# Moving the query copies ahead of a sine piece on GpSimd in a fused linear-attention and MLP kernel, with four smaller reorderings

## The chip, the cores and the metric

The kernel runs on one core of one Trainium2 chip. The metric is the device time of one execution in microseconds (us), as the median of several runs. A run's span in the profile is about 1.8 us shorter than its device time, because the profile counts from the first to the last instruction.

The engines are called as the profile calls them: PE is TensorE, DVE is VectorE, ACT is ScalarE, POOL (or Pool) is GpSimd, and SP issues the output stores. All five run at once, each in its own program order. They wait for one another only through semaphores.

## The reference

```python
# q, k, v: [8 batches, 8 heads, 576 positions, 64]
r = maximum(x, 0);  phi(x) = concat(r * cos(theta), r * sin(theta))   # theta grows with position
kv  = sum_s phi(k)[s] (x) v[s];  z = sum_s phi(k)[s]
x   = (phi(q) @ kv) / (phi(q) @ z + 1e-6)          # [4608, 512]
out = softplus(x @ w_in) @ w_out                   # w_in [512, 2048], w_out [2048, 512]
```

The kernel folds `w_in @ w_out` into one 512 x 512 matrix `W_c` and a bias, since softplus is almost linear for so small an argument. It checks the bound for that at the end; the check needs one sum of squares per tile, called norm `i`, which ScalarE computes, or VectorE for the tiles listed in `NORMS_DVE`. After the fold each of the 36 tiles of 128 tokens costs a few short PE groups.

## The kernel before

Per batch there is preparation: the values `v` are scaled by cos and by sin (`vcs`), the keys go through relu, and the queries are copied into another order (`q_r`). VectorE scales all cos pieces; the sin pieces are divided between VectorE and Pool. Then PE sums the key products of the batch. Per tile `i` there is the following, with PE's groups in this order:

```python
attend(i)          # PE: num_ps += qT[i] x kvblk;  DVE: rden = 1/den, x = num * rden
transpose(i - 1)   # PE: xT_ps <- x
keys(b)            # PE: 72 matmuls kv_ps <- vcs, k_sb, in the tile before the batch's first
emit(i - 4)        # PE: o_ps <- W_c, xT_all;  DVE: o_sb = o_ps + bias;  SP: store
turn(i + 2)        # PE: qT_ps <- diag, q_r (2 matmuls per query half);  ACT: qT = relu(qT_ps)
# then what the schedule has put into slot i, the end of tile i's work: prepare(...) of a later batch
```

The preparation that the change touches (cut; "..." marks cuts):

```python
def values_pool(b, hp, behind):          # one sin piece on Pool, 128 x 576
    ins = POOL.tensor_mul(vcs_bufs[b % 2][:, hp, :, 1, 0:D], raw["v", b][:, hp]..., cs_tab[:, 1])
    follow(ins, behind)                  # Pool waits until instruction `behind` has ended

def prepare(b, n):                       # slot first[b] - 6 + n for batches from 4 on
    if b < 4:
        ...
    else:
        if n < 3:
            relu_k(b) if n == 2 else values(b, 0, 2 * n)
        values_pool(b, n, None if n == 3 else before)   # before: the latest output add
        if n > 1:
            order_q(b, n - 2, POOL)      # query half n - 2, 128 x 576 int32
    if n == (2 if b < 4 else 3) and b + 3 < B:
        for name in ("v", "k", "q"):
            load(name, b + 3)
```

The output tiles `o_sb` form a ring of `OUTS = 16`, so output add n + 16 needs store n to have landed. The first stores are held back for loads:

```python
AHEAD = [("q", 5), ("v", 6), ("k", 6), ("q", 6), ("v", 7), ("k", 7)]   # store i waits for load AHEAD[i]
```

## Time and profile before

| | before |
|---|---|
| device time, median of 3 runs | 140.41 us (140.26 to 142.16) |
| span of the profile | 138.9 us |
| busy: PE, DVE, ACT, POOL | 82%, 71%, 71%, 56% |
| granted TensorE clock | 0.985 of full speed |

The profile is of another execution, which took 140.84 us. No engine is full on average, and the DMA engines are full until about 107 us. The averages therefore do not name the bound; it has to be read stage by stage.

The tables below use one more number, the lead. For tile n it is the time at which PE starts the tile's `attend` group in the profile of before, less that time in another profile. Positive means that the other kernel is ahead by so much. The column "end" is the last tile, 35. The places where the lead changes are the places where time is won or lost.

### The profile page before, as it was taken

Reading aid. Unit: us, or ns where it says so; the run is one execution under the profiler, and the core shown is the slowest. Engines: PE = TensorE matmul, PEld = TensorE weight load, DVE = VectorE, ACT = ScalarE, POOL = GpSimd, SP = SyncE. Lnnn points to the kernel's source line nnn. Section 1 sums busy time; section 2 is a strip of 40 time slices with the busy share of each in tenths; the row PEclk is TensorE's granted clock in tenths of the full one; section 3 lists DMA queues with packets and bytes.
Section 4 is the critical chain, followed back from the end, with each engine's and each line's share of the span. In section 5 each row is a group of like instructions: output and inputs, shape, how many; then the busy total and the mean of one; then the engine's idle time right before and its main releaser. Section 6 shows DMA issues by size and latency. Waiting matters only on the chain. (4 is left out here: it accounts for less than half of the span.)

```text
span 138.9 us, 3838 instructions
## 1 busy us (share of the span) xinstructions
PE 114.2 (82%) x1544; PEld 77.3 (56%) x1562; DVE 98.4 (71%) x205; ACT 98.5 (71%) x182; POOL 77.3 (56%) x81
## 2 busy tenths in 40 slices
PE   0199989999996776899899699789979987999910
PEld 0035775545444465676677477567747756776500
DVE  5184384335999599599599949959994896789720
ACT  3497873999841767888979579749949876899400
POOL 6964069993392519578568986915893591000000
PEclk9999999999999999999999999999999999999995
DMA  1999999999999999999999999999999432123570
GB/s 11 177 208 206 207 194 204 206 206 209 207 207 209 207 207 208 213 204 208 207 210 205 207 240 239 240 239 265 389 389 393 153 146 88 75 103 119 216 249 5
DMA packets 22676, 28.06 MB, mean 202 GB/s; under 512 B 1152, under 2 KB 18560, under 8 KB 22656
## 3 DMA queue, kind: packets, MB, share of 16 engines
q0 software_dynamic: 16896, 18.35, 78.4%
q1 hardware_dynamic: 5760, 9.44, 18.5%
q8 instruction: 13, 0.21, 0.6%
q14 instruction: 7, 0.06, 0.1%
HBM read 36.70 MB, written 9.44 MB: 332 GB/s over the span
## 5 line engine op out<-in xcount | busy, mean ns | idle before, releaser
L38 ACT ACTIVATE qT<-qT_ps 128x1024 bf16<-128x1024 f32 (+1 forms) x37 | 36.9, 1003 | 17.0 <-PE qT_ps L38 16.8
L38 POOL TENSOR_TENSOR vcs<-v_sb,cs_tab 128x576 bf16<-128x576 bf16 x22 | 35.2, 1602 | 16.6 <-DVE o_sb L38 12.4
L38 PE MATMUL o_ps<-W_c,xT_all 128*128 128x512 bf16 (+1 forms) x134 | 35.5, 373 | 0.9 <-issue 0.3
L38 DVE TENSOR_TENSOR o_sb<-o_ps,b_bc 128x512 f32<-128x512 f32 (+1 forms) x37 | 24.7, 671 | 9.2 <-PE o_ps L38 8.8
L38 PE MATMUL qT_ps<-diag,q_r 128*128 128x256 bf16 x144 | 22.5, 273 | 7.2 <-POOL q_r L38 5.1
L38 DVE TENSOR_TENSOR x<-num_ps,rden 128x512 bf16<-128x512 f32 x36 | 24.9, 692 | 3.5 <-ACT junk L38 0.6
L38 PE MATMUL num_ps<-kvblk,qT 128*128 128x130 bf16 (+1 forms) x320 | 22.8, 220 | 0.8 <-ACT qT L38 0.6
L38 PEld LDWEIGHTS <-q_r 128*128 128x128 bf16 x144 | 13.5, 98 | 17.1 <-POOL q_r L38 6.7
L38 ACT COPY xT_all<-xT_ps 128x1024 bf16<-128x1024 bf16 (+1 forms) x19 | 18.3, 961 | 2.5 <-PE xT_ps L38 2.5
L38 DVE TENSOR_TENSOR vcs<-v_sb,cs_tab 128x1152 bf16<-128x1152 bf16 x21 | 19.8, 961 | 0.2 <-DMA v_sb<-in_v_dram 0.2
L38 PEld LDWEIGHTS <-xT_all 128*128 128x128 bf16 x148 | 12.9, 98 | 10.4 <-issue 0.8
L38 PEld LDWEIGHTS <-qT 128*128 128x128 bf16 (+1 forms) x320 | 17.0, 99 | 1.3 <-ACT qT L38 1.0
L38 ACT ACTIVATE junk<-x 128x512 bf16<-128x512 bf16 x26 | 16.3, 627 | 0.0
L38 PEld LDWEIGHTS <-ones_bf 128*128 128x128 bf16 x94 | 9.6, 103 | 11.0 <-issue 7.9
L38 PE MATMUL wc_ps<-w_out_sb,wT 128*128 128x512 bf16 x61 | 14.6, 379 | 0.1
L38 PE MATMUL xT_ps<-order,x 128*128 128x128 bf16 x144 | 13.9, 219 | 0.9 <-DVE rden L38 0.3
L38 ACT CAST kvblk<-kv_ps 64x520 bf16<-64x520 f32 x16 | 9.5, 594 | 6.5 <-PE kv_ps L38 6.4
L38 PE MATMUL busy_ps<-cs_tab,ones_bf 128*128 128x512 bf16 x17 | 6.7, 557 | 6.4 <-ACT cs_tab L38 6.3
L38 PE MATMUL kv_ps<-vcs,k_sb 64*64 64x130 bf16 x576 | 10.1, 221 | 1.8 <-DVE k_sb L38 1.8
L38 DVE COPY wT<-wT_ps 128x512 bf16<-128x512 bf16 x16 | 6.0, 418 | 7.5 <-PE wT_ps L38 4.2
L38 DVE RECIPROCAL rden<-num_ps 128x8 f32<-128x8 f32 x36 | 7.3, 202 | 5.7 <-PE num_ps L38 5.6
L38 PEld LDWEIGHTS <-x 128*128 128x128 bf16 x144 | 9.8, 97 | 2.4 <-issue 1.7
(62 smaller groups left out, 131.9 us busy)
## 6 DMA issues: line engine op xcount, KB each, us to landing
out_dram<-o_sb SPq DMA_DIRECT2D x32, 256.0 KB, 3.8
v_sb<-in_v_dram POOLq DMA_DIRECT2D x8, 576.0 KB, 15.8
k_sb<-in_k_dram POOLq DMA_DIRECT2D x8, 576.0 KB, 18.3
q_sb<-in_q_dram POOLq DMA_DIRECT2D x8, 576.0 KB, 20.4
w_in_sb<-in_moe_w_in_dram POOLq DMA_DIRECT2D x4, 512.0 KB, 16.7
w_out_sb<-in_moe_w_out_dram POOLq DMA_DIRECT2D x4, 512.0 KB, 18.6
out_dram<-o_sb SPq DMA_DIRECT2D x8, 128.0 KB, 2.6
```

Of the source, the lines that this page charges most:

```text
L38: return self.tc.keep_in_program_order(f(*args, **kwargs))
```

## The change

The intent is to shorten the wait of PE for the second query half, and to clear some small waits around batches 1 to 3. The diff, cut to its core (the comments are not in the kernel):

```diff
-    NORMS_DVE = (4, 6, 14, 18, 19, 23, 27, 28, 30, 32)
+    NORMS_DVE = (5, 10, 14, 18, 19, 23, 27, 28, 30, 32)
...
+    fold(2, 2)
     turn_weights(3, 0)
     sum_rows(2, DVE, 0, 1)
-    fold(2, 2)
+    fold(2, 3)
     turn_weights(3, 1)
-    fold(2, 3)
...
-    values(1, 0, 0)
-    values_pool(1, 2, None)
-    values(1, 0, 2)
-    values_pool(1, 3, None)
-    values(1, 1, 0)
+    for n in range(4):
+        values(1, n // 2, 2 * (n % 2))
...
+    at(4, prepare, 2, (2, 3))                  # batch 2: both Pool pieces in slot 4
+    at(6, prepare, 2, (), (0, 1), True)        #          both query halves and the loads in slot 6
+    at(8, values, 3, 0, 0)                     # batch 3: two scalings in slot 8
+    at(8, values, 3, 0, 2)
+    at(8, prepare, 3, (2,))
+    at(9, values, 3, 1, 0)
+    at(9, prepare, 3, (3,), (0,))
+    at(10, relu_k, 3)
+    at(10, prepare, 3, (), (1,), True)
+    for b in range(4, B):                      # batches 4 to 7
+        s0 = first[b] - 6
+        at(s0, values, b, 0, 0)
+        at(s0, prepare, b, (0,))               # prepare(b, Pool pieces, query halves, loads)
+        at(s0 + 1, values, b, 0, 2)
+        at(s0 + 1, prepare, b, (1,), (0,))
+        at(s0 + 2, relu_k, b)
+        at(s0 + 2, prepare, b, (2,), (1,))
+        at(s0 + 3, prepare, b, (3,), (), b + 3 < B)
...
-    at(10, next, parts)
+    at(11, next, parts)
```

More of the change, by code (lines that the diff above doesn't have):

```diff
@@ L561, in at, with prepare @@
         todo.setdefault(max(i, 4), []).append((f, args))
-    def prepare(b, n):
-        if b < 4:
-            if n == 3:
-                relu_k(b)
-            else:
-                done = values(b, n // 2, 2 * (n % 2))
-            if n < 2:
-                values_pool(b, 2 + n, before)
-            if n < 2 if b == 2 else n in (1, 2):
-                order_q(b, n if b == 2 else n - 1, POOL, behind=done)
-        else:
-            if n < 3:
-                relu_k(b) if n == 2 else values(b, 0, 2 * n)
-            values_pool(b, n, None if n == 3 else before)
-            if n > 1:
-                order_q(b, n - 2, POOL)
-        if n == (2 if b < 4 else 3) and b + 3 < B:
+    def prepare(b, pieces=(), queries=(), more=False):
+        for hp in pieces:
+            values_pool(b, hp, before)
+        for hq in queries:
+            order_q(b, hq, POOL)
+        if more:
             for name in ("v", "k", "q"):
                 load(name, b + 3)
-    for b in range(2, B):
-        for n in range(4):
-            at((4 if b == 2 else 8 if b == 3 else first[b] - 6) + n, prepare, b, n)
+    for n in range(3):
+        at(4 + n, values, 2, n // 2, 2 * (n % 2))
+    at(7, relu_k, 2)
+    at(4, prepare, 2, (2, 3))
[16 more added lines that the diff above has]
+        at(s0 + 3, prepare, b, (3,), (), b + 3 < B)
     parts = weight_limit()
-    at(10, next, parts)
+    at(11, next, parts)
     for i in range(4, NT):
```

## The prediction

> **What bounds the kernel now.** I first read the page's slices, to find the stages:
>
> ```profile
> span 138.9 us, 3838 instructions
> PE   0199989999996776899899699789979987999910
> DVE  5184384335999599599599949959994896789720
> POOL 6964069993392519578568986915893591000000
> PEclk9999999999999999999999999999999999999995
> DMA  1999999999999999999999999999999432123570
> ```
>
> A slice is 3.47 us. DMA is full from 3 to 104 us, yet TensorE (PE) is also at 80 to 99% from about 55 us on, at full clock. So I asked who waits for whom. The load semaphores' last events give landings: v1 37.3, k1 40.1, q1 43.0, q2 51.5, then one load per 2.85 us: q3 60.1, q4 68.6, q5 77.3, q6 87.6, q7 98.3. Pool's query copies start at 51.65 for batch 2 (an idle of 2.87 us that ended with the load), but at 63.4, 76.3, 87.8, 100.9 and 112.4 for batches 3 to 7. Up to 51.5 us the loads set the pace; after that each batch has landed 3 to 14 us before it is needed, and compute does.
>
> Next the chain that ended last; its stretch before the last batch:
>
> ```profile
> 110.75 1.65 POOL vcs L38
> 112.41 0.61 POOL q_r L38
> 113.01 1.68 POOL vcs L38
> 114.69 0.62 POOL q_r L38
> 115.30 0.05 issue
> 115.35 0.39 PE qT_ps L38 x2
> ```
>
> Four Pool instructions in a row end at a PE matmul; afterwards the chain is PE alone up to 132.6 us. The PE timeline shows the same wait once per batch (in brackets: idle before, and what ended it):
>
> ```profile
> 54.97 0.39 PE L38 MATMUL qT_ps<-diag,q_r 128*128 128x256 bf16 x2 [0.68 <-POOL q_r L38]
> 79.30 0.39 PE L38 MATMUL qT_ps<-diag,q_r 128*128 128x256 bf16 x2 [1.24 <-POOL q_r L38]
> 90.75 0.39 PE L38 MATMUL qT_ps<-diag,q_r 128*128 128x256 bf16 x2 [1.09 <-POOL q_r L38]
> 103.86 0.39 PE L38 MATMUL qT_ps<-diag,q_r 128*128 128x256 bf16 x2 [0.89 <-POOL q_r L38]
> 115.35 0.39 PE L38 MATMUL qT_ps<-diag,q_r 128*128 128x256 bf16 x2 [1.15 <-POOL q_r L38]
> ```
>
> The first two matmuls of such a turn run at once, the last two (second query half) wait. An unhindered turn takes 0.44 us from start to the next group's start; these take 1.29 (53.90 to 55.19), 1.85, 1.70, 1.50 and 1.76. The stalls are thus 0.85, 1.41, 1.26, 1.06 and 1.32 us, plus 0.19 for batch 3 (65.02): 6.1 us. Elsewhere PE runs tiles at 2.04 us each.
>
> Last, batch 1, from the timelines of VectorE (DVE), Pool and PE:
>
> ```profile
> 37.36 5.10 DVE L38 TENSOR_TENSOR vcs<-v_sb,cs_tab 128x1152 bf16<-128x1152 bf16 x3 [0.21 <-DMA v_sb<-in_v_dram]
> 38.65 2.51 POOL L38 TENSOR_TENSOR vcs<-v_sb,cs_tab 128x576 bf16<-128x576 bf16 x2
> 43.19 1.24 PE L38 MATMUL kv_ps<-vcs,k_sb 64*64 64x130 bf16 x72 [1.11 <-DVE k_sb L38]
> ```
>
> Three VectorE scalings took 5.10 us instead of 3 x 0.67 (pitch) because Pool's two lay across them; PE then waited 1.11 us for the keys' relu behind them.
>
> **What the Trainium skill says.** "SBUF — State Buffer", section "SBUF: two separate sides": VectorE and GpSimd share a port pair as an exclusive lock held for a whole instruction, against VectorE instructions with two SBUF inputs. The trace agrees: the median VectorE scaling is 0.751 us, the longest 3.756 us, over the two Pool pieces; a Pool piece is 1.27 us where VectorE is quiet and about 1.66 us where it isn't. "GPSIMD Engine Reference", section 3.1, has two-input work at 1.96 times VectorE's time; here 1.27 us for 576 elements against 0.75 for 1152 is 3.4 times per element, so the trace's durations are used. "DMA: Bandwidth & Descriptors", section "Issuing engines are not separate DMA queues": all transfers interleave on the same 16 engines. The trace agrees: loads come each 2.85 us without stores, each 3.5 us with them (k6 to q7).
>
> **The change, part by part.**
> (1) Batches 4 to 7. Pool's order was piece 0, 1, 2, query 0, piece 3, query 1; it becomes piece 0, 1, query 0, piece 2, query 1, piece 3. Query 1 moves ahead of one piece (1.65 us), which is more than any of the stalls. By batch: piece 1 starts at 72.45, 83.90, 97.00, 108.22. From there 1.65 + 0.62 + 1.66 + 0.62 = 4.55 us, and for batch 7 up to 0.25 us more for the add that piece 2 follows, give query 1's end: 77.0, 88.45, 101.55, 113.0. The unhindered second half of the turn would come 0.22 us after its first: 77.9, 89.5, 102.8, 114.0. All in time, by 0.9 to 1.3 us, so the whole 1.41 + 1.26 + 1.06 + 1.32 = 5.05 us of stalls goes.
> (2) Batch 2. Both pieces now run in slot 4, before q2 lands; then both queries at 51.65: end at about 53.2 (two of 0.66 to 0.89), not 54.91. The turn then waits only for ScalarE, which has one more norm (0.71 us) ahead of it: about 0.3 to 0.5 of the 0.85 us comes back here beyond what (3) brings. Batch 3: the second query no longer follows a VectorE scaling (0.19), and relu is a slot earlier (PE waited 0.40 for it at 66.94).
> (3) Batch 1 on VectorE alone: 4 x 0.67 = 2.7 us from about 38.0 (its row sums come 0.6 later, because the last weight block is turned later), relu done by 41.4, not 43.1. PE's wait of 1.11 goes. But q1 lands at 43.0 and two copies take 0.88, so the turn starts at about 44.1, not 45.23: 1.1 us.
> (4) Later weight turn: one group of four 0.22-us folds moves ahead. PE had waits of 0.05 and 0.18 us here and gets about as much elsewhere: 0.
> (5) Two scalings in slot 8 beside a Pool piece: the second can be locked out for up to 1.27 us; norm 10 comes to VectorE (0.68) while norms 4 and 6 leave. VectorE had 1.4 us idle after it (67.8 to 69.5), so I let this cost 0.3 to 1.0 us.
> Sum before batch 4: 1.1 + 0.4 + 0.6 - 0.7 = 1.4 us. With (1), 6.4 us, if nothing else stops it.
>
> **Rivals.**
> (a) The output ring takes its place. There are 16 output tiles, so add n+16 needs store n landed, and the first stores are held for loads, which the change can't speed up. Store landings against the adds that need them: store 3 93.48 and 98.42; store 4 97.44 and 100.61; store 5 98.96 and 102.91; store 6 99.62 and 107.39. The tightest slack is 100.61 - 97.44 = 3.17 us, at add 20. By then the gain is 1.4 + 1.41 + 1.26 = 4.1 us, so VectorE waits some 0.9 us there; PE's next output group had 0.4 us of slack (add end 101.29, group start 101.72), so PE loses about 0.5. I count this in. It would also cap any larger gain up to that point at about 3.6, after which batches 6 and 7 still add 2.4: about 6.0 at most.
> (b) The third sine piece, now last and behind an add, holds up the key products. It ends 1.7 us after query 1: 78.7, 90.15, 103.25, 114.7; the products would start at 79.1, 90.5, 104.1, 115.1 and need that piece only in their second half, 0.6 us on. It fits by 0.4 us or more. If it slipped by 1 us each time, 2 us would return: 137.0.
> (c) VectorE becomes the bound. Between batches it idles 1.98, 1.87, 2.49 and 1.88 us (mostly waits for PE after the stall); less the stalls, 0.57, 0.61, 1.43 and 0.56 us remain. It fits, with little to spare; if port conflicts add 0.5 us a batch, 1 to 2 us are lost: 136 to 137.
> (d) The transfers bind: then nothing is won. Against it: from batch 3 on loads are early, and the tail (DMA at 10 to 50%) is PE's.
>
> **Range and chances.** 6.4 - 0.5 for the ring is 5.9. For (b) and (c), which are each tight in every batch, I take off 0.7, which is a choice: 5.2 us, so 140.4 - 5.2 = 135.2 us, 3.7% faster. Low, 133.8: all stalls go, and neither (b), (c) nor much of (5) costs anything. High, 137.4: half of the stalls return as (b) or (c). Slower than that needs both. Two per cent is 137.6 us: faster 0.85, within 0.13, slower 0.02.
>
> **What would show it.** Right: PE's idle ended by Pool's q_r nearly gone in batches 4 to 7; the chain PE (with some VectorE) where it had Pool; key products in batch 1 near 42.1 us; no VectorE scaling of 3.7 us; a wait of VectorE's output add for an output store near 97.5 us; the span's last 17 us as before, only earlier. Wrong: idle before the key products ended by Pool's vcs (b); PE waiting for VectorE's x in most tiles (c); or the adds from 97 to 100 us waiting for stores by more than 1.5 us (a larger than counted).

## The result

The changed kernel took 135.97 us (median of 4 runs, 135.71 to 136.24), against 140.49 us for the kernel before in the same rounds. The ratio is 0.9653, with a 95% interval of 0.9576 to 0.973, so it is 3.5% faster. Ratios here are the mean time of one kernel's fast runs over that of the other's of the same rounds, so they are not quite the ratio of the medians that are quoted. All runs gave correct results.

The page of the changed kernel, its slices:

```profile
span 134.1 us, 3835 instructions
PE   0199989999899975896999999999999999999910
POOL 6973139996223376553938999954895791000000
DMA  1999999999999999999999999999999983233670
```

A slice is now 3.35 us. From about 67 us on PE is at 90% or more in every slice but the last two, where it had dips to 60, 70 and 80% before. DMA is full for as long as before: the loads did not get faster, and they did not need to.

The PE timeline at the four turns that answer to those of 79.30, 90.75, 103.86 and 115.35 us:

```profile
77.94 0.60 PE L38 MATMUL qT_ps<-diag,q_r 128*128 128x256 bf16 x4
88.12 0.60 PE L38 MATMUL qT_ps<-diag,q_r 128*128 128x256 bf16 x4
100.17 0.60 PE L38 MATMUL qT_ps<-diag,q_r 128*128 128x256 bf16 x4
110.34 0.60 PE L38 MATMUL qT_ps<-diag,q_r 128*128 128x256 bf16 x4
```

Each turn is now one group of four matmuls with no idle bracket, where before the last two stood apart behind a wait for Pool. Pool's timeline for batch 7 shows why; its columns are start, busy time, engine, line, operation (L38 is a helper's line, which nearly all instructions have):

```profile
104.74 1.65 POOL L38 TENSOR_TENSOR vcs<-v_sb,cs_tab 128x576 bf16<-128x576 bf16 x1 [1.67 <-DVE o_sb L38]
106.34 0.66 POOL L38 COPY q_r<-q_sb 128x576 int32<-128x576 int32 x1
107.07 1.68 POOL L38 TENSOR_TENSOR vcs<-v_sb,cs_tab 128x576 bf16<-128x576 bf16 x1
108.70 0.66 POOL L38 COPY q_r<-q_sb 128x576 int32<-128x576 int32 x1
109.32 1.72 POOL L38 TENSOR_TENSOR vcs<-v_sb,cs_tab 128x576 bf16<-128x576 bf16 x1
```

The second query copy ends at 109.36 us, 1.2 us before the turn's second half would want it (110.34 + 0.22). The last piece ends at 111.04 us, and the key products start at 111.61 us. In the chain that ended last, the same stretch holds no Pool at all:

```profile
109.91 0.59 PE o_ps L38 x2
110.50 0.44 PE qT_ps L38 x4
110.94 0.51 PE num_ps L38 x10
111.45 0.22 PE xT_ps L38 x4
111.68 1.17 PE kv_ps L38 x54
```

Batch 1 also came out as meant. VectorE's four scalings take the time of four, and the key products follow PE's output groups with no gap:

```profile
37.73 2.76 DVE L38 TENSOR_TENSOR vcs<-v_sb,cs_tab 128x1152 bf16<-128x1152 bf16 x4
42.07 1.25 PE L38 MATMUL kv_ps<-vcs,k_sb 64*64 64x130 bf16 x72
```

But in slot 8, where the change puts two scalings, VectorE, Pool and PE show this:

```profile
58.48 2.50 DVE L38 TENSOR_TENSOR vcs<-v_sb,cs_tab 128x1152 bf16<-128x1152 bf16 x2
58.65 1.72 POOL L38 TENSOR_TENSOR vcs<-v_sb,cs_tab 128x576 bf16<-128x576 bf16 x1 [2.78 <-DVE o_sb L38]
61.95 0.40 PE L38 MATMUL xT_ps<-order,x 128*128 128x128 bf16 x4 [1.12 <-DVE x L38]
```

Before, this slot had one scaling of 0.75 us, and PE did not wait for `x`:

```profile
59.42 0.75 DVE L38 TENSOR_TENSOR vcs<-v_sb,cs_tab 128x1152 bf16<-128x1152 bf16 x1
61.61 0.39 PE L38 MATMUL xT_ps<-order,x 128*128 128x128 bf16 x4
```

The two scalings take 2.50 us for the 1.4 that two take when undisturbed. The second is shut out until Pool's piece has ended at 60.37 us. PE then waits 1.12 us for VectorE's `x`.

The leads put all this on one scale. The stalled turns are those of tiles 18, 22, 27 and 31, the first of batches 4 to 7. PE does each just before it attends to tile 17, 21, 26 and 30, so the stall of a batch shows between two neighbouring columns.

| lead of the changed kernel (us) at tile | 4 | 9 | 11 | 13 | 17 | 21 | 26 | 30 | end |
|---|---|---|---|---|---|---|---|---|---|
| after | 1.12 | 0.95 | -0.71 | -0.20 | 1.15 | 2.41 | 3.48 | 4.80 | 4.78 |

Batch 1 brings 1.1 us, 0.2 us of it is gone by tile 9, slot 8 takes 1.66 us, and batch 3's earlier relu gives 0.5 us back. At tile 13, before the first batch with the new order, the changed kernel is 0.20 us behind. Then come four steps of 1.35, 1.26, 1.07 and 1.32 us, in sum 5.00 us.

### The profile page after: what moved, and what is told of

The parts are those of the page before. It is cut to its first block, busy times and chain, and to the rows that moved or that the text cites. A ratio compares the mean times of both kernels' runs of the same rounds, so it can differ in the third digit from the quotient of the medians.

```text
span 134.1 us, 3835 instructions
## 1 busy us (share of the span) xinstructions
PE 113.7 (85%) x1544; PEld 77.4 (58%) x1562; DVE 97.5 (73%) x206; ACT 99.0 (74%) x182; POOL 74.6 (56%) x79
## 2 busy tenths in 40 slices
DMA packets 22676, 28.06 MB, mean 209 GB/s; under 512 B 1152, under 2 KB 18560, under 8 KB 22656
## 4 chain that ended last, share of the span: by engine, by line
PE 60%; ACT 14%; DVE 10%; POOL 6%; issue 5%; POOLq 0%; ACTq 0%; DVEq 0%
PE o_ps L38 17%; PE wc_ps L38 9%; PE qT_ps L38 7%; PE num_ps L38 6%; PE kv_ps L38 6%; ACT qT L38 5%; PE busy_ps L38 5%; PE xT_ps L38 4%; ACT xT_all L38 4%; ACT junk L38 3%; PE wT_ps L38 3%; DVE vcs L38 3%; DVE x L38 3%; POOL vcs L38 3%; DVE wT L38 1%
## 5 line engine op out<-in xcount | busy, mean ns | idle before, releaser
L38 ACT ACTIVATE qT<-qT_ps 128x1024 bf16<-128x1024 f32 (+1 forms) x37 | 36.9, 1003 | 12.7 <-PE qT_ps L38 12.4
L38 POOL TENSOR_TENSOR vcs<-v_sb,cs_tab 128x576 bf16<-128x576 bf16 x20 | 32.9, 1650 | 13.9 <-DVE o_sb L38 9.9
L38 PE MATMUL o_ps<-W_c,xT_all 128*128 128x512 bf16 (+1 forms) x134 | 35.5, 373 | 1.1 <-issue 0.3
L38 DVE TENSOR_TENSOR o_sb<-o_ps,b_bc 128x512 f32<-128x512 f32 (+1 forms) x37 | 24.7, 672 | 8.5 <-PE o_ps L38 8.0
L38 DVE TENSOR_TENSOR x<-num_ps,rden 128x512 bf16<-128x512 f32 x36 | 24.9, 692 | 3.1 <-ACT junk L38 0.6
L38 PE MATMUL num_ps<-kvblk,qT 128*128 128x130 bf16 (+1 forms) x320 | 22.8, 220 | 0.8 <-ACT qT L38 0.6
L38 PE MATMUL qT_ps<-diag,q_r 128*128 128x256 bf16 x144 | 21.6, 272 | 1.9 <-ACT qT L38 1.7
L38 ACT COPY xT_all<-xT_ps 128x1024 bf16<-128x1024 bf16 (+1 forms) x19 | 18.3, 962 | 2.9 <-PE xT_ps L38 2.9
L38 PEld LDWEIGHTS <-q_r 128*128 128x128 bf16 x144 | 13.8, 98 | 10.4 <-issue 2.4
L38 PEld LDWEIGHTS <-xT_all 128*128 128x128 bf16 x148 | 13.0, 97 | 10.9 <-issue 1.1
L38 DVE TENSOR_TENSOR vcs<-v_sb,cs_tab 128x1152 bf16<-128x1152 bf16 x22 | 18.6, 871 | 0.0
L38 PEld LDWEIGHTS <-qT 128*128 128x128 bf16 (+1 forms) x320 | 17.0, 99 | 1.3 <-ACT qT L38 1.0
L38 PE MATMUL xT_ps<-order,x 128*128 128x128 bf16 x144 | 13.9, 219 | 3.0 <-DVE x L38 2.3
L38 ACT ACTIVATE junk<-x 128x512 bf16<-128x512 bf16 x26 | 16.2, 626 | 0.0
L38 PEld LDWEIGHTS <-ones_bf 128*128 128x128 bf16 x94 | 9.6, 103 | 11.1 <-issue 8.0
L38 PE MATMUL wc_ps<-w_out_sb,wT 128*128 128x512 bf16 x61 | 14.6, 379 | 0.4 <-DVE wT L38 0.3
L38 ACT CAST kvblk<-kv_ps 64x520 bf16<-64x520 f32 x16 | 9.5, 594 | 4.9 <-PE kv_ps L38 4.8
L38 PEld LDWEIGHTS <-x 128*128 128x128 bf16 x144 | 9.6, 97 | 4.9 <-DVE x L38 2.9
L38 DVE COPY wT<-wT_ps 128x512 bf16<-128x512 bf16 x16 | 6.0, 418 | 8.4 <-PE wT_ps L38 4.2
L38 PE MATMUL busy_ps<-cs_tab,ones_bf 128*128 128x512 bf16 x17 | 6.7, 555 | 6.4 <-ACT cs_tab L38 6.3
L38 ACT ACTIVATE junk<-wT 128x512 bf16<-128x512 bf16 x16 | 9.8, 620 | 0.6 <-DVE wT L38 0.4
L38 PE MATMUL kv_ps<-vcs,k_sb 64*64 64x130 bf16 x576 | 10.0, 218 | 0.3 <-DVE k_sb L38 0.3
```

The lines of the kernel that those rows point to most:

```text
L38: return self.tc.keep_in_program_order(f(*args, **kwargs))
```

## The experiments

Eleven kernels were run, the first four (order_alone, order_undone, slot8_spread, ring_14) on another chip than the rest, each beside the kernel before. The theory was: the whole gain is the four stalls; what the other parts win for batch 1 is spent in slot 8; the output ring of 16 tiles does not bind at this lead, but is near. The rivals: the other parts carry a share; the ring or the loads have set the result; the loss in slot 8 is VectorE's load, not the lock.

The leads of all of them, from their profiles:

| lead (us) at tile | 4 | 9 | 11 | 13 | 17 | 21 | 26 | 30 | end |
|---|---|---|---|---|---|---|---|---|---|
| order_alone | 0.20 | 0.20 | 0.20 | 0.20 | 1.47 | 2.75 | 3.82 | 5.14 | 5.14 |
| order_undone | 0.79 | 0.85 | -0.81 | -0.31 | -0.23 | -0.23 | -0.23 | -0.03 | -0.06 |
| slot8_spread | 1.14 | 0.92 | 0.92 | 0.31 | 1.66 | 2.92 | 4.00 | 5.31 | 5.29 |
| ring_14 | 0.89 | 1.00 | -0.66 | -0.15 | 1.19 | 2.17 | 0.24 | 1.56 | 1.53 |
| slot8_behind | 1.16 | 0.99 | 0.41 | 0.92 | 2.27 | 3.54 | 4.61 | 5.92 | 5.90 |
| slot4_apart | 0.95 | 1.16 | -0.50 | 0.01 | 1.36 | 2.63 | 3.70 | 5.02 | 4.99 |
| batch1_undone | 0.20 | 0.42 | -1.24 | -0.73 | 0.61 | 1.89 | 2.95 | 4.27 | 4.24 |
| combo | 1.16 | 1.40 | 1.10 | 1.24 | 2.52 | 3.79 | 3.73 | 5.05 | 5.05 |
| combo_17 | 1.33 | 1.16 | 1.16 | 1.17 | 2.45 | 3.72 | 4.79 | 6.11 | 6.11 |
| behind_apart_16 | 1.26 | 1.21 | 0.63 | 1.13 | 2.48 | 3.75 | 4.82 | 6.13 | 6.10 |
| behind_apart_17 | 0.76 | 1.24 | 0.66 | 1.17 | 2.51 | 3.78 | 4.85 | 6.17 | 6.14 |

A row holds one profiled execution. From one execution to another the first tiles shift by 0.2 to 0.5 us, so differences below that at tile 4 say nothing. Ratios are to the kernel before in the same rounds.

### order_alone: the new order and nothing else

The kernel before, with this edit:

```diff
-            values_pool(b, n, None if n == 3 else before)
-            if n > 1:
-                order_q(b, n - 2, POOL)
+            values_pool(b, n, before)
+            if n in (1, 2):
+                order_q(b, n - 1, POOL)
```

> The kernel before with only the order of Pool's work for batches 4 to 7 changed (piece 0, 1, query 0, piece 2, query 1, piece 3). If the four second-half query stalls (1.41 + 1.26 + 1.06 + 1.32 us) are all that this part touches, the time falls by 5.05 us, to 135.4 us, and at output add 20 the lead is 2.7 us, below the 3.17 us of slack before the output ring binds, so VectorE waits for no store there. This would be as fast as the whole change or faster. Rival: the other parts of the change carry a share of the gain, and this alone gives 3.5 us or less (137 us or more).

Measured: 135.70 us (135.53 to 135.85), ratio 0.9659 (0.9642 to 0.9676). Before had 140.54 us in these rounds. The lead rises by 1.27, 1.28, 1.07 and 1.32 us at the four places, 4.94 us together. This one edit is as fast as the whole change.

### order_undone: all but the new order

The changed kernel, with the old order for batches 4 to 7:

```diff
-        at(s0 + 1, prepare, b, (1,), (0,))
+        at(s0 + 1, prepare, b, (1,), ())
...
-        at(s0 + 2, prepare, b, (2,), (1,))
-        at(s0 + 3, prepare, b, (3,), (), b + 3 < B)
+        at(s0 + 2, prepare, b, (2,), (0,))
+        at(s0 + 3, values_pool, b, 3, None)
+        at(s0 + 3, prepare, b, (), (1,), b + 3 < B)
```

> The changed kernel with the old order of Pool's work for batches 4 to 7. If the other parts together bring nothing by the start of batch 4 (the two traces show PE 0.2 us later there), this is as slow as the kernel before: 140.3 to 141.0 us, with PE's idle for Pool's queries back at 0.9 to 1.25 us in four places. Rival: the other parts bring 1 us or more that shows only at the end: 139.5 us or less.

Measured: 140.85 us (140.63 to 140.99), ratio 1.0025 (1.0007 to 1.0043). The waits of PE from 60 us on, as engine, what it waited for, us in total, times, longest:

```profile
PE qT_ps L38 <- POOL q_r L38: 4.1, 4, 1.2
PE xT_ps L38 <- DVE x L38: 1.1, 1, 1.1
```

The four waits are back, and the wait for `x` of slot 8 stands beside them. So the other parts together bring nothing at the end; with order_alone, this settles the first rival.

### ring_14: two output tiles fewer

```diff
-    LOADS, OUTS = 15, 16
+    LOADS, OUTS = 15, 14
```

> The changed kernel with 14 output tiles for 16. Add n+14 then waits for store n: add 18 (now at 93.8 us) for store 4, which landed at 97.3. If landings are set by the loads and not by compute, VectorE waits 3.5 us there and PE loses that less its slack: the time rises by 2.5 to 3.5 us, to 138.5 to 139.5 us, with a VectorE wait that ends with an output store between 90 and 98 us. Rival: the ring has no part in this kernel: 136.0 us and no such wait.

Measured: 139.61 us (139.16 to 139.94), ratio 0.9942 (0.9923 to 0.9961), just above the stated range. VectorE's adds waited four times, 4.2 us in all; the longest of them:

```profile
94.43 0.69 DVE L38 TENSOR_TENSOR o_sb<-o_ps,b_bc 128x512 f32<-128x512 f32 x1 [2.60 <-DMA out_dram<-o_sb]
97.28 0.69 DVE L38 TENSOR_TENSOR o_sb<-o_ps,b_bc 128x512 f32<-128x512 f32 x1 [0.65 <-DMA out_dram<-o_sb]
```

These are adds 17 and 18. Store 3 landed at 94.34 and store 4 at 97.19 us, each 0.09 us before the add that needed it. I had named add 18 alone; most of the wait falls one add earlier. The lead drops from 2.17 to 0.24 us between tiles 21 and 26, where the others gain 1.07. So the ring is a real bound, two tiles away from the changed kernel. Store 4 landed between 96.6 and 97.7 us in every profile but one, with leads from -0.2 to 3.8 us at tile 21, so it does not follow compute. Its issue follows the load for which it is held: `v` of batch 7 landed at 91.10 us before and 91.21 us after, and store 4 was issued 0.06 us later in both.

### slot8_spread: one scaling per slot again

```diff
     at(8, values, 3, 0, 0)
-    at(8, values, 3, 0, 2)
     at(8, prepare, 3, (2,))
-    at(9, values, 3, 1, 0)
+    at(9, values, 3, 0, 2)
     at(9, prepare, 3, (3,), (0,))
-    at(10, relu_k, 3)
+    at(10, values, 3, 1, 0)
     at(10, prepare, 3, (), (1,), True)
+    at(11, relu_k, 3)
```

> The changed kernel with batch 3's VectorE work spread over slots 8 to 11 again (one scaling each in 8, 9 and 10, relu in 11). PE lost 1.65 us between tiles 10 and 11, where it waited 1.12 us for x behind the second scaling of slot 8. If that is lost for good, the time falls by 1.65 us, less 0.4 us for the later relu and up to 0.5 us at output add 20, where the lead of some 4 us is over the 3.17 us of slack: 134.8 to 135.3 us. Rival: VectorE's total load limits this stretch, so that the time is caught up again by the keys of batch 3 in either kernel: 135.8 to 136.2 us, as the whole change.

Measured: 135.47 us (135.28 to 135.58), ratio 0.9642 (0.9624 to 0.9659), between the two expectations. The loss at tile 11 is gone (0.92 for -0.71), but most of it comes back at the keys of batch 3:

```profile
66.63 1.24 PE L38 MATMUL kv_ps<-vcs,k_sb 64*64 64x130 bf16 x72 [1.13 <-DVE k_sb L38]
```

I had allowed 0.4 us for the later relu. It stood behind norm 10, which the change had moved to VectorE in the same slot, so it was 1.13 us. In combo, below, with that norm back on ScalarE, it is 0.50 us. The two scalings in slot 8 and the early relu belong together: the early relu is what the two scalings buy.

### slot8_behind: two scalings in slot 8, Pool after them

```diff
     at(8, values, 3, 0, 0)
-    at(8, values, 3, 0, 2)
-    at(8, prepare, 3, (2,))
+    at(8, lambda: values_pool(3, 2, values(3, 0, 2)))
```

> The changed kernel, with both scalings still in slot 8, but Pool's piece made to follow the second scaling, so that Pool can't lock VectorE out of it. In the changed kernel the second scaling ended 1.1 us late behind Pool's piece, and PE waited 1.12 us for x. If the lock is what slot 8 costs, VectorE does the two scalings in 1.4 us for 2.5, PE's wait for x goes, and since batch 3's relu stays early, the lead at tile 13 rises by about 1 us: 134.8 to 135.2 us. Rival: it is the second scaling's own 0.67 us in that slot, not the lock: 135.6 us or more, with a wait for x of over 0.5 us left.

Measured: 134.93 us (134.72 to 135.14), ratio 0.9584 (0.9542 to 0.9626); before had 140.75 us in these rounds. Both scalings now take the time of two:

```profile
58.44 1.42 DVE L38 TENSOR_TENSOR vcs<-v_sb,cs_tab 128x1152 bf16<-128x1152 bf16 x2
```

PE's wait for `x` is gone, and the lead at tile 13 is 0.92 us where the changed kernel has -0.20. At tile 11 the lead is 0.41 us for -0.71, so the lock accounts for 1.12 us of the 1.66; the remaining 0.54 us is what the second scaling itself costs there: it has 0.67 us of its own, and slot8_spread, without it, loses nothing between tiles 9 and 11 (0.92 at both). "SBUF — State Buffer" of the Trainium skill (section "SBUF: two separate sides") describes this lock, and the run agrees: the same instructions on the same engines cost 1.1 us less when the order keeps them apart.

### slot4_apart: the two Pool pieces of batch 2 apart

```diff
-    for n in range(3):
+    at(4, prepare, 2, (2,))
+    at(4, lambda: values_pool(2, 3, values(2, 0, 0)))
+    for n in (1, 2):
         at(4 + n, values, 2, n // 2, 2 * (n % 2))
     at(7, relu_k, 2)
-    at(4, prepare, 2, (2, 3))
```

> The changed kernel with Pool's second piece of batch 2 made to follow VectorE's scaling of slot 4, not run directly behind its first piece. VectorE's scaling there took 2.30 us for 0.75, and PE waited 0.67 + 0.16 + 0.29 us for x and 0.27 us for the keys. If these waits are worth their length, the time falls by 0.5 to 1.0 us (135.0 to 135.5 us). Rival: ScalarE's turns and the landing of the queries of batch 2 pace this stretch, so only the waits behind the last turn (0.29 + 0.27) count: 0.5 us at most, or nothing (135.5 to 136.0 us).

Measured: 135.85 us (135.56 to 135.92), ratio 0.9641 (0.9599 to 0.9682). The rival holds. PE's waits for `x` before tile 9 went, but the lead at tile 9 rose only from 0.95 to 1.16 us. That is small, but the five kernels with this edit have 1.16 to 1.40 us there, and five otherwise like them but without it 0.85 to 1.00 us. Before the turns of tiles 6 to 9 PE waits for ScalarE in both kernels (idle of 0.38 to 0.60 us where it shows), so a wait for `x` removed there becomes a wait for ScalarE: in slot4_apart PE waits 0.40 us for ScalarE's `xT_all` before tile 8, where it waited 0.16 us for `x`.

### batch1_undone: batch 1 with two pieces on Pool again

```diff
-    for n in range(4):
-        values(1, n // 2, 2 * (n % 2))
+    values(1, 0, 0)
+    values_pool(1, 2, None)
+    values(1, 0, 2)
+    values_pool(1, 3, None)
+    values(1, 1, 0)
```

> The changed kernel with batch 1 scaled as before, two pieces of it on Pool. The lock on VectorE comes back (three scalings in 5.1 us), PE waits 1.1 us for the keys of batch 1. If that wait is passed on, the time rises by 0.7 to 1.1 us, to 136.7 to 137.1 us. Rival: the landing of the queries of batch 2 at 51.4 us sets the pace behind it anyhow, and the lead of batch 1 is lost there: 136.0 to 136.3 us.

Measured: 136.81 us (136.57 to 137.49), ratio 0.973 (0.9682 to 0.9779), within the range. By medians that is 0.84 us slower than the changed kernel, in other rounds; by the leads of the two profiles it is 0.9 us at tile 4 and 0.53 us from tile 9 on. So 0.5 to 0.8 us of batch 1's 0.9 us is passed on, and the rest is lost on the way to tile 9, most likely where ScalarE paces, which no run here isolates.

### combo: the first three repairs together

This is slot8_spread with slot 4's edit of slot4_apart and norm 10 back on ScalarE:

```diff
-    NORMS_DVE = (5, 10, 14, 18, 19, 23, 27, 28, 30, 32)
+    NORMS_DVE = (5, 14, 18, 19, 23, 27, 28, 30, 32)
```

> The changed kernel with batch 3 spread over slots 8 to 11, norm 10 back on ScalarE, and Pool's second piece of batch 2 behind the scaling of slot 4. In slot8_spread PE waited 1.13 us for the keys of batch 3, behind norm 10 (0.68 us) and the relu on VectorE; without the norm about 0.4 us should stay, and slot 4 adds up to 0.5 us: a lead of 1.0 to 1.5 us at tile 13 where slot8_spread had 0.3. At output add 20 that makes 3.6 to 4.1 us, over the 3.17 us of slack, so a wait of VectorE for a store of 0.4 to 0.9 us should appear near 97.5 us, and PE loses at most 0.5 us of it: 134.3 to 134.9 us. Rival: the leads before batch 4 don't add up to the end: 135.3 us or more.

Measured: 134.75 us median of 6 (134.63 to 135.99), ratio 0.9564 (0.9524 to 0.9603). The median is in the range, and so is the lead at tile 13. The profiled run took 135.63 us, and it shows the ring at work. The VectorE and PE timelines:

```profile
98.32 0.69 DVE L38 TENSOR_TENSOR o_sb<-o_ps,b_bc 128x512 f32<-128x512 f32 x1 [1.33 <-DMA out_dram<-o_sb]
99.07 1.02 PE L38 MATMUL o_ps<-W_c,xT_all 128*128 128x512 bf16 x4 [0.97 <-DVE o_sb L38]
```

This is add 20. Both waits are longer than expected (0.4 to 0.9 us, and 0.5 us at most). Store 4 was issued at 91.16 us as usual but landed at 98.23 us in this execution, the one late case (why, the trace does not say), and the lead fell by 0.06 us where it otherwise rises by 1.07. Four of the six runs took 134.63 to 134.80 us, so it does not cost that much in all of them; they have no profile.

### combo_17, behind_apart_16 and behind_apart_17: one output tile more

combo_17 is combo with `OUTS = 17`. The other two are the changed kernel with both Pool pieces put behind VectorE's scalings (the edits of slot8_behind and slot4_apart), with 16 and with 17 output tiles.

> The kernel combo with 17 output tiles for 16, so that output add 21, not add 20, needs store 4. In combo's profile add 20 waited 1.33 us for store 4 and PE 0.97 us behind it, and its lead fell from 3.79 to 3.73 us where the other kernels gain 1.07. Add 21 comes some 2.2 us later, so with one tile more no add should wait for a store, and the lead at the end is 1.24 + 5.0 = 6.2 us: 134.0 to 134.4 us. Rival: the wait moves to another add or the lead is lost elsewhere: 134.7 us or more.

> The changed kernel with both Pool pieces made to follow VectorE's scalings (those of slot8_behind and of slot4_apart), 16 output tiles. The leads add up to 0.92 + 0.21 = 1.1 us at tile 13 and 3.7 us at add 20, against a slack of 3.2 to 3.6 us over the landings seen for store 4 (96.9 to 97.4 us; before's add 20 at 100.6): a store wait of 0 to 0.6 us, all or most of it within PE's own slack of 0.4 us: 134.6 to 135.0 us.

> The same with 17 output tiles: no store wait at add 20, a lead of 1.1 + 5.0 = 6.1 us at the end: 134.2 to 134.6 us, 0.1 to 0.5 us under its pair with 16. Rival: the ring doesn't bind at a lead of 3.7 us, and the two are equal.

Measured, with 5 rounds and before at 140.72 us:

| | median us (of 6) | range | ratio | add 20 starts | store 4 landed |
|---|---|---|---|---|---|
| combo_17 | 134.66 | 134.50 to 135.13 | 0.9564 (0.9531 to 0.9597) | 96.98 | 96.72 |
| behind_apart_16 | 134.72 | 134.52 to 134.95 | 0.9568 (0.9538 to 0.9598) | 96.95 | 96.62 |
| behind_apart_17 | 134.77 | 134.44 to 135.12 | 0.9573 (0.954 to 0.9607) | 96.92 | 96.76 |

combo_17 ended with about the lead that was expected (6.11 us for 6.2), but its time is 0.26 us above the range I gave: I had taken the lead from 140.4 us, and before ran at 140.72. behind_apart_17 missed its range by 0.17 us: the pair with 16 and 17 tiles is equal, as its rival said. With 16 tiles add 20 came 0.33 us after store 4, so it did not wait for that store. The ring was touched one add later:

```profile
99.59 0.69 DVE L38 TENSOR_TENSOR o_sb<-o_ps,b_bc 128x512 f32<-128x512 f32 x1 [0.25 <-DMA out_dram<-o_sb]
```

This is add 21 of behind_apart_16, 0.10 us after store 5 landed (99.49 us). PE did not wait behind it: the lead rises by 1.07 us from tile 21 to 26, as with 17 tiles. slot8_behind shows the same with 0.18 us. So at this lead a ring of 16 tiles already makes VectorE wait, inside PE's slack. That the seventeenth tile helps in the executions in which store 4 lands late is likely from combo's profile, but no run of mine shows it: the two worst runs of combo (135.63 and 135.99 us) have no counterpart in the twelve runs with 17 tiles, and none in the six of behind_apart_16 either. This stays open.

## Why the prediction was right

The forecast was 135.2 us (133.8 to 137.4), the measurement 135.97 us. The main step held almost exactly, and smaller steps missed in both directions. Of the signs named for it, all appeared but the wait for an output store near 97.5 us; in the chain that ended last, Pool gave way to PE with ScalarE (22% of it from 68 us on), where some VectorE was expected. Two readings of the first view were loose, and nothing rests on them: DMA is full until about 107 us, not 104, and PE's slices from 55 us on have dips to 60 and 70%.

**Part (1), the four stalls.** Forecast 5.05 us, measured 5.00 us in the changed kernel and 4.94 us in order_alone. Reading the stall as the turn's length less the undisturbed 0.44 us was sound, and so was the check that nothing else would wait in its place.

**Rival (b), the last sine piece.** It fitted. The last pieces ended at 78.95, 89.11, 100.88 and 111.04 us, and the key products started at 79.42, 89.39, 101.65 and 111.61 us, without a wait.

**Rival (c), VectorE as the bound.** From 60 us on PE waited for VectorE's `x` once, for 1.1 us, and that was slot 8. In batches 4 to 7 it did not. The 0.7 us that the forecast took off for (b) and (c) was not needed.

**Rival (a), the ring.** The reading was right in kind: ring_14 and combo show it, and store landings hardly depend on compute. Its 0.5 us did not come due, since the lead at add 20 was 2.4 us, not 4.1.

**The step that was mis-sized: the sum before batch 4.** The forecast had a lead of 1.4 us there; it was -0.20. Batch 1 held (1.12 us for 1.1) and batch 3 nearly (0.51 us for 0.6, though its turn, at 65.57 us, still waits for the second query and is 0.75 us long for 0.63 before). Two terms of that sum failed. For part (5) the forecast allowed 0.3 to 1.0 us (0.7 in the sum); slot 8 cost 1.66 us between tiles 9 and 11. I had counted the lock of up to 1.27 us and set VectorE's idle time further on against it, and that idle time was no help: it lies behind the keys, while PE needed `x` at once. The second scaling's own 0.67 us in that slot was left out as well; slot8_behind and slot8_spread show these two costs as 1.1 and 0.5 us. For batch 2 in part (2) the forecast had 0.3 to 0.5 us more than batch 1's; instead the lead fell from 1.12 to 0.95 us at tile 9. Two Pool pieces back to back made VectorE's scaling in slot 4 take 2.30 us for 0.75, which the forecast never priced:

```profile
46.99 2.51 POOL L38 TENSOR_TENSOR vcs<-v_sb,cs_tab 128x576 bf16<-128x576 bf16 x2
47.83 2.30 DVE L38 TENSOR_TENSOR vcs<-v_sb,cs_tab 128x1152 bf16<-128x1152 bf16 x1
```

slot4_apart shows that the lock itself costs only 0.2 us there. The turns wait for ScalarE in any case; the other 0.4 us of this miss was not taken apart.

So 1.6 us too much before batch 4 was mostly offset by 1.2 us of deductions that were not needed. The total was good to 0.8 us, partly by that balance, which is luck. By the profiles it was good to 0.4 us (4.8 us for 5.2); most of the rest is that before's profiled execution took 140.84 us, against medians of 140.4 to 140.5.

**What stays open.** The later turn of the weight block, the moves of norms 4, 5 and 6, and the later pair of query copies of batch 2 were not run alone. The output groups after the fold start at 40.18 us before and 40.25 us after, which fits a worth of nothing for the weight turn, but that was only read from the traces.

**A better kernel.** combo_17, at 134.66 us, behind_apart_16 at 134.72 and behind_apart_17 at 134.77 us are the fastest, some 4.3% under the kernel before and 0.9% under the changed one by medians. They can't be told apart; behind_apart_16 is the smallest edit, two dependencies.

## What to carry to other kernels

When the bounding engine waits in the same place once per period, look at the order of the helper engine's work ahead of it: putting what is needed first in front is free if what moves back still comes before its own need (here by 0.28 us in the tightest batch). Price a lock between two engines by where the shut-out engine's next result is needed, not by that engine's idle time later on. Before counting on a gain, compare the new lead with the slack of every ring of buffers whose releases are tied to transfers, since those do not move along.

## What the Trainium skill lacked or had wrong

- "SBUF — State Buffer", section "SBUF: two separate sides": it says that the loser is blocked for a whole instruction. It does not say what happens when the winner issues a second one directly behind. Here VectorE's scaling waited for both of two back-to-back Pool pieces (46.99 to 49.50 us) and took 2.30 us for 0.75.
- "GPSIMD Engine Reference", section 3.1: its two-input comparison is for fp32 (1.96 times VectorE's time). For the bf16 products of this kernel an undisturbed Pool piece took 1.27 us for 576 elements against 0.75 us for 1152 on VectorE, 3.4 times per element.
- "DMA: Bandwidth & Descriptors", section "Anatomy of one DMA — SWDGE (gpsimd) path": its fit of a fixed 2.0 us plus bytes over bandwidth is for a DMA on the software path, and I found no figure for a hardware-queue store beside a full software queue. In the changed kernel store 4 (256 KB) took 6.0 us from issue (91.27) to landing (97.28) beside the loads, and store 27 took 2.4 us (116.62 to 118.98) without them. That latency, and the holding of the first stores for loads, bring the output ring near to binding.
